# Two fixed places for keys and one for values instead of three in turn, in a cached attention step with a gated feed-forward

## The chip, the cores and the metric

The kernel runs on 1 core of one Trainium2 chip. The metric is the device time of one execution in microseconds (us). The core has a matrix engine (TensorE, PE in the profile), a vector engine (VectorE, DVE), a scalar engine (ScalarE, ACT), GpSimd (POOL), a synchronisation engine (SyncE, SP) that here only starts transfers, and 16 DMA engines that move the data. The on-chip memory has 128 partitions; a "place" below is 64 KB in each of them, 8 MB in all.

## What is computed

One decoding step: for two sequences (B = 2) with one new token each, attention over a cache of 4096 keys and values in 16 heads of 256 numbers, and beside it a feed-forward layer; a gate mixes the two.

```
q = (x @ wq).reshape(B, 1, 16, 256).transpose(0, 2, 1, 3)
scores = einsum("bhqd,bhkd->bhqk", q, k_cache) * 256 ** -0.5
p = softmax(scores);  o = einsum("bhqk,bhkd->bhqd", p, v_cache)
a = o.transpose(0, 2, 1, 3).reshape(B, 1, 4096) @ wo
h = relu(x @ w1 + b1) ** 2;  b = h @ w2 + b2
g = sigmoid((x * gate_w).sum(-1));  out = g * a + (1 - g) * b
```

All numbers are 32-bit floats. The two caches hold 134 MB each; x has 448 numbers per sequence, wq is 448 x 4096, wo is 4096 x 448, w1 is 448 x 1792 and w2 is 1792 x 448.

## The kernel before

The attention is done in 16 **rounds**. A round is a pair of heads `t` (0 to 7) of one sequence `b` (0 or 1), in the order (0,0), (0,1), (1,0) and so on. The keys of a round are 2 x 4096 rows of 256 numbers; laid over 128 partitions, 64 keys in each, they fill one place, and so do the values of the round. Each cache tensor is moved once.

**Places.** A pool `ring` with three places (L51) is handed out in turn, one place for each call of `place` (L62), whatever is to be put there: wq, the keys of round 0, wf (w1 and w2 together), the keys of round 1, and then values and keys alternately. The order of the calls thus fixes which tile follows which in a place: the values of round r come into the place of the keys of round r, and the keys of round r+2 into the place of the values of round r-1. A load into a place waits until the last reader of what stood there is done. All large loads are issued by SP, in the order of the program; a load that waits holds up those behind it. The DMA engines take the issued loads in order. ACT issues two small loads, `pack` (x, the gate's weights and b1 in 28 columns, L83) and b2 (L88), on a queue of its own.

**Start.** wq comes in two loads (L80), the keys of round 0 and of round 1 in four loads each (`cut4`, L84), wf in two (L89, L90). PE multiplies x with wq (`project_q`, L151), and `make_q(r)` (L166) spreads the q of one round over the partitions.

**A round** (loop from L278). `scores(r)` (L179): DVE multiplies the keys with q in place (L184) and sums over the 256 numbers (L185), in quarters for rounds 0 and 1, whole after that. Then SP issues the values of this round (L281), and PE makes q of the next one. `values(r - 1)` (L217) has PE multiply the weights p of the round before with its values in 64 steps; after every second round `turn` (L226) brings the result, with its normalisation, into columns `oT` that can be multiplied with wo. Then the keys of round r+2 are issued (L295), and `softmax(r)` (L187) takes the maximum, spreads it by PE, and has ACT make p. `norm` (L205) works out the normalisation after every second round. In round 0 `ffn` (L245), the feed-forward layer, follows the softmax.

**End.** wo is loaded in five pieces of 16, 8, 4, 3 and 1 blocks (`cuts`, L277) into the place of the last keys. Each block of 128 rows is multiplied with its `oT` columns. The first 28 blocks are added by `add` (L139) into the accumulator `acc`, which holds four partial sums in four groups of rows. ACT copies `acc` to `ya` (L314). The last four blocks (`LATE = 4`, L135) go by `late` (L145) straight into a second accumulator `fin`, after `ya` has been folded into it with the selection matrix `pick` (L315); `wide` (L119, L312) holds their `oT` columns spread out. ACT copies `fin` to `y4` (L318), and SP stores it (L319).

Of the kernel before, what the change touches and what calls it, by code (L numbers as in the profile page):

```python
# [19 lines left out]
def kernel(  # L20
# [24 lines left out]
    DQ = D // 4  # L45
    PLACE = KEYS * DH
    W = 17
    scale = DH ** -0.5

    const = ctx.enter_context(tc.tile_pool(name="const", bufs=1))  # L50
    ring = ctx.enter_context(tc.tile_pool(name="ring", bufs=3))  # L51
    work = ctx.enter_context(tc.tile_pool(name="work", bufs=2))
    solo = ctx.enter_context(tc.tile_pool(name="solo", bufs=1))
    ps = ctx.enter_context(tc.tile_pool(name="ps", bufs=2, space=PSUM))
# [4 lines left out]
    rounds = [(t, b) for t in range(T) for b in range(B)]  # L59
    R = len(rounds)  # L60

    def place(name):  # L62
        return ring.tile([P, PLACE], F32, name=name, tag="ring")

    def load(t, src, lo, hi):
        nc.sync.dma_start(t[:, lo:hi], src[:, lo:hi])  # L66

    def load_kv(cache, r, name, cuts=()):
        t, b = rounds[r]
        tl = place(f"{name}{r}")  # L70
        src = cache[b, 2 * t:2 * t + 2].rearrange("h (p j) d -> (h p) (j d)", j=KEYS)
        at = [0, *cuts, KEYS]
        for lo, hi in zip(at, at[1:]):
            load(tl, src, lo * DH, hi * DH)
        return tl.rearrange("p (j d) -> p j d", d=DH)

    kt, vt = {}, {}

    wqt = place("wq")
    for lo, hi in ((0, 2 * N), (2 * N, 3 * N + N // 2)):  # L80
        load(wqt, wq, lo, hi)
    pk = const.tile([P, 28], F32, name="pk")
    nc.scalar.dma_start(pk, pack)  # L83
    cut4 = (KEYS // 4, KEYS // 2, 3 * KEYS // 4)  # L84
    kt[0] = load_kv(k_cache, 0, "k", cut4)
    wft = place("wf")
    b2r = wft[0:1, PLACE - D:]
    nc.scalar.dma_start(b2r, b2)  # L88
    load(wft, wf, 0, CF * F + F // 2)  # L89
    load(wft, wf, CF * F + F // 2, CF * F + F // 2 + FC * D)  # L90
    kt[1] = load_kv(k_cache, 1, "k", cut4)

    ident = const.tile([P, P], F32, name="ident")
    make_identity(nc, ident)
# [9 lines left out]
    fin = ps1.tile([P, 512], F32, name="fin")  # L104
# [11 lines left out]
    pick = const.tile([P, W], F32, name="pick")  # L116
    nc.vector.memset(pick, 0.0)
    nc.vector.tensor_copy(pick[:, 0:W:16], m8[:, :2])
    wide = const.tile([P, 4, W], F32, name="wide")  # L119
    nc.vector.memset(wide, 0.0)  # L120

    xT = pk[:, :10].rearrange("p (c b) -> p c b", b=B)
# [12 lines left out]
    LATE = 4  # L135
    n_acc = 1 + FC + T * 4 - LATE
    added = [0]

# [6 lines left out]
    def late(lt, rhs, start=False, stop=False):  # L145
        for k in range(4):
            nc.tensor.matmul(fin[32 * k:32 * k + W, :DQ], lt, rhs[:, k * DQ:(k + 1) * DQ], start=start, stop=stop)  # L147
# [16 lines left out]
    q_sb = {}  # L164
# [11 lines left out]

    s_t = {}

    def scores(r, cuts=()):  # L179
        s_t[r] = work.tile([P, KEYS], F32, name=f"s{r}", tag="s")  # L180
        at = [0, *cuts, KEYS]
        for lo, hi in zip(at, at[1:]):
            k = kt[r][:, lo:hi, :]
            nc.vector.tensor_tensor(k, k, q_sb[r].unsqueeze(1).to_broadcast([P, hi - lo, DH]), op=ALU.mult)  # L184
            nc.vector.tensor_reduce(s_t[r][:, lo:hi], k, axis=AX.X, op=ALU.add)  # L185

    def softmax(r):  # L187
        t, b = rounds[r]
        m = work.tile([P, 1], F32, name=f"m{r}", tag="m")
        nc.vector.tensor_reduce(m, s_t[r], axis=AX.X, op=ALU.max)  # L190
        mt = ps.tile([P, 512], F32, name=f"mt{r}", tag="sm")
        nc.tensor.matmul(mt[:, :P], m.to_broadcast([P, P]), ident, start=True, stop=True)  # L192
        nb = work.tile([P, 1], F32, name=f"nb{r}", tag="nb")
        for hh in range(2):
            z = slice(64 * hh, 64 * hh + 64)
            nc.vector.tensor_reduce(nb[z], mt[z, z], axis=AX.X, op=ALU.max, negate=True)  # L196
# [41 lines left out]

    def o_block(t, k):
        hh, j = divmod(k, 2)  # L240
        return oT[t][:, j, :, hh]
# [3 lines left out]
    def ffn():  # L245
        ph = ps.tile([P, 512], F32, name="ph", tag="pq")
        for c in range(CF + 1):
            for n in range(4):
                if c < CF:
                    lt, at = xT[:, c, :], c * F + n * D  # L250
                else:
                    half, m = divmod(n, 2)
                    lt, at = xT[:, CF + half, :], CF * F + m * D
                nc.tensor.matmul(ph[32 * n:32 * n + B, :D], lt, wft[:, at:at + D], start=(c == 0), stop=(c == CF))  # L254
        w2_at = CF * F + F // 2
        h_at = w2_at + FC * D
# [12 lines left out]
        add(gP[0:1, 1, :], b2r)  # L269
        for c in range(FC):  # L270
            add(hT[:, c, :], wft[:, w2_at + c * D:w2_at + (c + 1) * D])

    project_q()
    make_q(0)
    half15 = (KEYS // 2, 3 * KEYS // 4, 7 * KEYS // 8)
    blocks = [(t, k) for t in WO_ORDER for k in range(4)]
    cuts = (0, 16, 24, 28, 31, 32)  # L277
    for r, (t, b) in enumerate(rounds):  # L278
        scores(r, cut4 if r < 2 else ())
        if r < R - 1:  # L280
            vt[r] = load_kv(v_cache, r, "v")  # L281
            make_q(r + 1)
        else:
            wot = place("wo")
            for lo, hi in zip(cuts, cuts[1:]):
                load(wot, wo, lo * D, hi * D)
        if r > 0:
            values(r - 1)
            if b == 0:
                turn(t - 1)  # L290
        if r == 0:
            softmax(r)
            ffn()
        if r + 2 < R:
            kt[r + 2] = load_kv(k_cache, r + 2, "k")  # L295
        elif r + 2 == R:
            vt[R - 1] = load_kv(v_cache, R - 1, "v", half15)
        if r > 0:
            softmax(r)
        if b == B - 1:  # L300
            norm(t)
    values(R - 1)
    turn(T - 1)
    for i, (t, k) in enumerate(blocks):
        rhs = wot[:, i * D:(i + 1) * D]
        if i < len(blocks) - LATE:
            add(o_block(t, k), rhs)
            continue
        n = i - (len(blocks) - LATE)
        if n == 0:  # L310
            for kk in range(LATE):
                nc.vector.tensor_copy(wide[:, kk, 0:W:16], o_block(t, kk))  # L312
            ya = const.tile([P, D], F32, name="ya")
            nc.scalar.activation(ya, acc[:, :D], AF.Copy)  # L314
            late(pick, ya, start=True)  # L315
        late(wide[:, n, :], rhs, stop=n == LATE - 1)
    y4 = const.tile([P, DQ], F32, name="y4")
    nc.scalar.activation(y4, fin[:, :DQ], AF.Copy)  # L318
    nc.sync.dma_start(out.rearrange("b s (k n) -> k (b s) n", k=4), y4[0:P:16, :])  # L319


# [58 lines left out]
```

## Time and profile before

| | us |
|---|---|
| median of 3 runs | 684.85 |
| fastest and slowest of the three | 683.78 and 685.77 |
| the profiled execution's own time | 685.27 |
| its span in the profile | 683.5 |
| DVE busy | 572.1 |
| PE busy | 216.6 |
| ACT busy | 33.2 |

The trace covers the span; the profiled execution's own time lies 1.8 us above it. Busy shares are averages over the span. Times in the rows of the trace are counted from the span's start. A line number is that of the code of the kernel that the row belongs to. A transfer's time to landing runs from its issue, so it holds the time in the queue as well.

### The profile page before, as it was taken

What the parts mean: (1) busy time and instruction counts of PE and PEld (TensorE: products, weight loads), DVE (VectorE), ACT (ScalarE), POOL (GpSimd) and SP (SyncE); (2) the same over time, 40 slices, a digit from 0 to 9 for tenths busy, and PEclk for the clock granted to TensorE, in tenths of its full rate; (3) what the DMA queues carried; (4) which work ended last, traced back from release to release, by engine and by line L of the source; (5) the groups of instructions that cost most, each with busy time, mean ns of one, the idle gap of its engine ahead of it and who ended that gap; (6) DMA issues with size and microseconds to landing.
All of it is one profiled execution on the core that took longest, in us unless ns stands there. A gap on an engine that the chain in (4) does not pass through costs nothing.

```text
span 683.5 us, 3411 instructions
## 1 busy us (share of the span) xinstructions
PE 216.6 (32%) x1452; PEld 62.5 (9%) x1452; DVE 572.1 (84%) x148; ACT 33.2 (5%) x107; POOL 0.7 (0%) x6
## 2 busy tenths in 40 slices
PE   2304441150515133060514215061412406050366
PEld 0001100010101001010100101010100101010012
DVE  2595895979989798989989798997979799897950
ACT  0101000010000000010000100000000100000000
POOL 0000000000000000000000000000000000000000
PEclk9756766565657556575656656575755756575579
DMA  9999999999999999999999999999999999999996
GB/s 383 420 435 423 434 433 454 445 437 426 427 403 433 433 434 430 430 431 433 433 426 434 433 433 433 437 427 418 434 414 433 395 433 434 422 430 419 419 425 278
DMA packets 7372, 289.77 MB, mean 424 GB/s; under 512 B 957, under 2 KB 1086, under 8 KB 1342
## 3 DMA queue, kind: packets, MB, share of 16 engines
q1 hardware_dynamic: 7212, 289.54, 98.9%
q8 instruction: 11, 0.18, 0.1%
q10 hardware_dynamic: 146, 0.02, 0.0%
q14 instruction: 3, 0.02, 0.0%
HBM read 289.55 MB, written 0.00 MB: 424 GB/s over the span
## 4 chain that ended last, share of the span: by engine, by line
DMA 50%; DVE 46%; PE 2%; issue 1%; ACT 0%; SPq 0%; DVEq 0%; ACTq 0%
DMA k<-in_k_cache_dram 47%; DVE s L185 23%; DVE k L184 23%; DMA wo<-in_wo_dram 3%; PE acc L142 1%; PE ph L254 1%; PE pt L263 0%; DVE m L190 0%; SPq L66 0%; PE mt L192 0%; PE fin L147 0%; ACT p L200 0%; ACT ya L314 0%; ACT wf L259 0%; DVEq L184 0%
## 5 line engine op out<-in xcount | busy, mean ns | idle before, releaser
L184 DVE TENSOR_TENSOR k<-k,q 128x16384 f32<-128x16384 f32 (+1 forms) x22 | 276.5, 12568 | 41.8 <-DMA k<-in_k_cache_dram 31.4
L185 DVE TENSOR_REDUCE s<-k 128x64 f32<-128x16384 f32 (+1 forms) x22 | 276.4, 12566 | 0.8
L223 PE MATMUL po<-v,p 128*8 128x512 f32 x1024 | 147.2, 740 | 318.8 <-DMA v<-in_v_cache_dram 318.8
L223 PEld LDWEIGHTS po<-v,p 128*8 128x8 f32 x1024 | 29.4, 104 | 433.1 <-issue 262.7
L192 PE MATMUL mt<-ident,m 128*128 128x128 f32 x32 | 12.0, 477 | 111.0 <-DVE m L190 111.0
L200 ACT ACTIVATE p<-s,nb 64x64 f32<-64x64 f32 x32 | 11.2, 350 | 368.1 <-DVE nb L196 367.7
L196 DVE TENSOR_REDUCE nb<-mt 64x1 f32<-64x64 f32 x32 | 7.1, 222 | 15.3 <-PE mt L192 14.8
L192 PEld LDWEIGHTS mt<-ident,m 128*128 128x128 f32 x32 | 7.8, 303 | 119.0 <-issue 82.7
L172 PE MATMUL pq<-qs,ident 128*64 128x256 f32 x64 | 16.0, 600 | 0.0
L228 ACT ACTIVATE o<-po 128x512 f32<-128x512 f32 x8 | 4.8, 597 | 216.4 <-PE po L223 216.4
L210 DVE RECIPROCAL rc<-sum 128x4 f32<-128x4 f32 x8 | 1.5, 183 | 11.0 <-PE sum L207 11.0
L234 PE MATMUL ot<-rl,o 128*128 128x4 f32 x64 | 8.4, 255 | 6.2 <-ACT o L228 6.2
L234 PEld LDWEIGHTS ot<-rl,o 128*128 128x128 f32 x64 | 7.7, 191 | 13.7 <-ACT o L228 13.7
L160 PE MATMUL po<-wq,pk 128*2 128x512 f32 x64 | 8.6, 683 | 1.3 <-DMA wq<-in_wq_dram 1.3
L207 PE MATMUL sum<-rsm,ones 128*128 128x4 f32 x16 | 4.5, 351 | 10.3 <-ACT p L200 10.3
L125 DVE TENSOR_TENSOR y<-pk 128x8 f32<-128x8 f32 x1 | 0.2, 168 | 9.1 <-DMA pk<-in_pack_dram 9.1
L175 ACT ACTIVATE q<-pq 128x256 f32<-128x256 f32 x16 | 6.1, 383 | 20.4 <-PE pq L172 20.2
L265 DVE TENSOR_TENSOR hb<-pt,pk 128x28 f32<-128x28 f32 x1 | 0.2, 188 | 8.1 <-PE pt L263 8.1
L142 PE MATMUL acc<-wo,oT 128*2 128x448 f32 x56 | 5.8, 538 | 1.1 <-DMA wo<-in_wo_dram 1.1
L200 ACT ACTIVATION_READ_ACCUMULATOR p<-s,nb 64x1 f32 x32 | 5.9, 184 | 0.0
L207 PEld LDWEIGHTS sum<-rsm,ones 128*128 128x128 f32 x16 | 3.8, 294 | 12.6 <-ACT p L200 12.6
L142 PE MATMUL acc<-wf,hT 128*2 128x448 f32 x28 | 4.9, 812 | 0.1
(49 smaller groups left out, 45.0 us busy)
## 6 DMA issues: line engine op xcount, KB each, us to landing
k<-in_k_cache_dram SPq DMA_DIRECT2D x8, 2048.0 KB, 35.7
wf<-in_wf_dram SPq DMA_DIRECT2D x2, 3136.0 KB, 37.8
wq<-in_wq_dram SPq DMA_DIRECT2D x1, 4096.0 KB, 12.2
v<-in_v_cache_dram SPq DMA_DIRECT2D x1, 4096.0 KB, 33.5
wo<-in_wo_dram SPq DMA_DIRECT2D x1, 3584.0 KB, 13.7
wq<-in_wq_dram SPq DMA_DIRECT2D x1, 3072.0 KB, 19.1
v<-in_v_cache_dram SPq DMA_DIRECT2D x1, 2048.0 KB
v<-in_v_cache_dram SPq DMA_DIRECT2D x2, 1024.0 KB, 40.8
```

What stands on the lines that cost most here:

```text
L142: nc.tensor.matmul(acc[32 * g:32 * g + B, :D], lt, rhs, start=n < 4, stop=n >= n_acc - 4)
L160: nc.tensor.matmul(po_bufs[a][32 * gq:32 * gq + B, :], lt, wqt[:, at:at + QB], start=(c == 0), stop=(c == CF))
L172: nc.tensor.matmul(pq[64 * hh:64 * hh + 64, :DH], ident[:, row:row + 1].to_broadcast([P, 64]), qs[:, a, hh * DH:(hh + 1) * DH], start=True ...
L184: nc.vector.tensor_tensor(k, k, q_sb[r].unsqueeze(1).to_broadcast([P, hi - lo, DH]), op=ALU.mult)
L185: nc.vector.tensor_reduce(s_t[r][:, lo:hi], k, axis=AX.X, op=ALU.add)
L192: nc.tensor.matmul(mt[:, :P], m.to_broadcast([P, P]), ident, start=True, stop=True)
L196: nc.vector.tensor_reduce(nb[z], mt[z, z], axis=AX.X, op=ALU.max, negate=True)
L200: nc.scalar.activation(p8[b][z, :, c:c + 3:2], s_t[r][z].rearrange("p (m s) -> p m s", s=2), AF.Exp, bias=nb[z], accum_out=rsm[t % 2][z, h ...
L207: nc.tensor.matmul(sm[:, :4], ones.to_broadcast([P, P]), rsm[t % 2].rearrange("p h b -> p (h b)"), start=True, stop=True)
L223: nc.tensor.matmul(po[g:g + 8, :], p8[b][:, m, :], v[:, m, :], start=(b == 0 and m < 4), stop=(b == B - 1 and m >= NM - 4))
L234: nc.tensor.matmul(ptv[:, j, :], o[:, at:at + P], rl_t[t][:, s].rearrange("p b h -> p (b h)"), start=(s == 0), stop=(s == 1))
L254: nc.tensor.matmul(ph[32 * n:32 * n + B, :D], lt, wft[:, at:at + D], start=(c == 0), stop=(c == CF))
```

## The change

- The pool `ring` with three places becomes a pool `keys` with two and a pool `vals` with one. wq, all keys and the values of the last round take turns in `keys`; wf, the values of rounds 0 to 14 and wo follow one another in the one place of `vals`. The memory taken is the same.
- The order of the issues in a round changes with it: the values of round r are issued after `values(r - 1)`, which frees their place, and then the keys of round r+2. wo is issued after `values(14)`. The load of the keys of round 1 moves behind `project_q` and `make_q(0)` in the program.
- wq comes in one load, the keys of rounds 0 and 1 in one load each, the last values in two (three quarters and one) instead of four. `pack` is loaded in two halves and b2 in four pieces.
- `scores` is split into `times_q` and `row_sums`, both over the whole tile; in round 0 `ffn` stands between them and the softmax comes after them.
- `LATE` becomes 8: 24 blocks of wo go into `acc`, eight straight into `fin`. The spread columns for all eight are made ahead of the additions. The first late block starts `fin`, and `ya` is folded in after four of them. The last copy of `fin` is made by DVE instead of ACT.

```diff
-    ring = ctx.enter_context(tc.tile_pool(name="ring", bufs=3))
+    keys = ctx.enter_context(tc.tile_pool(name="keys", bufs=2))
+    vals = ctx.enter_context(tc.tile_pool(name="vals", bufs=1))
...
-    wqt = place("wq")
-    for lo, hi in ((0, 2 * N), (2 * N, 3 * N + N // 2)):
-        load(wqt, wq, lo, hi)
+    wqt = place(keys, "wq")
+    load(wqt, wq, 0, 3 * N + N // 2)
     pk = const.tile([P, 28], F32, name="pk")
-    nc.scalar.dma_start(pk, pack)
-    cut4 = (KEYS // 4, KEYS // 2, 3 * KEYS // 4)
-    kt[0] = load_kv(k_cache, 0, "k", cut4)
-    wft = place("wf")
+    for z in (slice(0, 14), slice(14, 28)):
+        nc.scalar.dma_start(pk[:, z], pack[:, z])
+    kt[0] = load_kv(k_cache, 0, keys, "k")
+    wft = place(vals, "wf")
     b2r = wft[0:1, PLACE - D:]
-    nc.scalar.dma_start(b2r, b2)
+    for k in range(4):
+        nc.scalar.dma_start(b2r[:, k * DQ:(k + 1) * DQ], b2[:, k * DQ:(k + 1) * DQ])
     load(wft, wf, 0, CF * F + F // 2)
     load(wft, wf, CF * F + F // 2, CF * F + F // 2 + FC * D)
-    kt[1] = load_kv(k_cache, 1, "k", cut4)
...
-    def scores(r, cuts=()):
+    def times_q(r):
+        nc.vector.tensor_tensor(kt[r], kt[r], q_sb[r].unsqueeze(1).to_broadcast([P, KEYS, DH]), op=ALU.mult)
+
+    def row_sums(r):
         s_t[r] = work.tile([P, KEYS], F32, name=f"s{r}", tag="s")
...
+        nc.vector.tensor_reduce(s_t[r], kt[r], axis=AX.X, op=ALU.add)
...
     project_q()
     make_q(0)
-    half15 = (KEYS // 2, 3 * KEYS // 4, 7 * KEYS // 8)
+    kt[1] = load_kv(k_cache, 1, keys, "k")
...
     for r, (t, b) in enumerate(rounds):
-        scores(r, cut4 if r < 2 else ())
+        times_q(r)
         if r < R - 1:
-            vt[r] = load_kv(v_cache, r, "v")
             make_q(r + 1)
-        else:
-            wot = place("wo")
-            for lo, hi in zip(cuts, cuts[1:]):
-                load(wot, wo, lo * D, hi * D)
+        if r == 0:
+            ffn()
+        row_sums(r)
         if r > 0:
             values(r - 1)
             if b == 0:
                 turn(t - 1)
-        if r == 0:
-            softmax(r)
-            ffn()
+        if r < R - 1:
+            vt[r] = load_kv(v_cache, r, vals, "v")
+        else:
+            wot = place(vals, "wo")
+            for lo, hi in zip(cuts, cuts[1:]):
+                load(wot, wo, lo * D, hi * D)
         if r + 2 < R:
-            kt[r + 2] = load_kv(k_cache, r + 2, "k")
+            kt[r + 2] = load_kv(k_cache, r + 2, keys, "k")
         elif r + 2 == R:
-            vt[R - 1] = load_kv(v_cache, R - 1, "v", half15)
-        if r > 0:
-            softmax(r)
+            vt[R - 1] = load_kv(v_cache, R - 1, keys, "v", (3 * KEYS // 4,))
+        softmax(r)
...
+    early = len(blocks) - LATE
+    for n, (t, k) in enumerate(blocks[early:]):
+        nc.vector.tensor_copy(wide[:, n, 0:W:16], o_block(t, k))
     for i, (t, k) in enumerate(blocks):
...
         if n == 0:
-            for kk in range(LATE):
-                nc.vector.tensor_copy(wide[:, kk, 0:W:16], o_block(t, kk))
             ya = const.tile([P, D], F32, name="ya")
             nc.scalar.activation(ya, acc[:, :D], AF.Copy)
-            late(pick, ya, start=True)
-        late(wide[:, n, :], rhs, stop=n == LATE - 1)
+        if n == LATE // 2:
+            late(pick, ya)
+        late(wide[:, n, :], rhs, start=n == 0, stop=n == LATE - 1)
     y4 = const.tile([P, DQ], F32, name="y4")
-    nc.scalar.activation(y4, fin[:, :DQ], AF.Copy)
+    nc.vector.tensor_copy(y4, fin[:, :DQ])
```

More of the change, by code (lines that the diff above doesn't have):

```diff
@@ L60, with place, load_kv @@
     R = len(rounds)
-    def place(name):
-        return ring.tile([P, PLACE], F32, name=name, tag="ring")
+    def place(pool, name):
+        return pool.tile([P, PLACE], F32, name=name, tag="place")
     def load(t, src, lo, hi):
         nc.sync.dma_start(t[:, lo:hi], src[:, lo:hi])
-    def load_kv(cache, r, name, cuts=()):
+    def load_kv(cache, r, pool, name, cuts=()):
         t, b = rounds[r]
-        tl = place(f"{name}{r}")
+        tl = place(pool, f"{name}{r}")
         src = cache[b, 2 * t:2 * t + 2].rearrange("h (p j) d -> (h p) (j d)", j=KEYS)
@@ L118 @@
     nc.vector.tensor_copy(pick[:, 0:W:16], m8[:, :2])
-    wide = const.tile([P, 4, W], F32, name="wide")
+    LATE = 8
+    wide = const.tile([P, LATE, W], F32, name="wide")
     nc.vector.memset(wide, 0.0)
@@ L133 @@
     nc.vector.tensor_scalar(gP[:, 1, :], gP[:, 0, :], -1.0, 1.0, op0=ALU.mult, op1=ALU.add)
-    LATE = 4
     n_acc = 1 + FC + T * 4 - LATE
@@ L177 @@
     s_t = {}
-    def scores(r, cuts=()):
+    def times_q(r):
+        nc.vector.tensor_tensor(kt[r], kt[r], q_sb[r].unsqueeze(1).to_broadcast([P, KEYS, DH]), op=ALU.mult)
+    def row_sums(r):
         s_t[r] = work.tile([P, KEYS], F32, name=f"s{r}", tag="s")
[L181 to L185, printed above, removed]
+        nc.vector.tensor_reduce(s_t[r], kt[r], axis=AX.X, op=ALU.add)
     def softmax(r):
@@ L303 @@
     turn(T - 1)
+    early = len(blocks) - LATE
+    for n, (t, k) in enumerate(blocks[early:]):
+        nc.vector.tensor_copy(wide[:, n, 0:W:16], o_block(t, k))
     for i, (t, k) in enumerate(blocks):
         rhs = wot[:, i * D:(i + 1) * D]
-        if i < len(blocks) - LATE:
+        if i < early:
             add(o_block(t, k), rhs)
             continue
-        n = i - (len(blocks) - LATE)
+        n = i - early
         if n == 0:
-            for kk in range(LATE):
-                nc.vector.tensor_copy(wide[:, kk, 0:W:16], o_block(t, kk))
             ya = const.tile([P, D], F32, name="ya")
             nc.scalar.activation(ya, acc[:, :D], AF.Copy)
-            late(pick, ya, start=True)
-        late(wide[:, n, :], rhs, stop=n == LATE - 1)
+        if n == LATE // 2:
+            late(pick, ya)
+        late(wide[:, n, :], rhs, start=n == 0, stop=n == LATE - 1)
     y4 = const.tile([P, DQ], F32, name="y4")
-    nc.scalar.activation(y4, fin[:, :DQ], AF.Copy)
+    nc.vector.tensor_copy(y4, fin[:, :DQ])
     nc.sync.dma_start(out.rearrange("b s (k n) -> k (b s) n", k=4), y4[0:P:16, :])
```

## The prediction

> **What bounds the kernel now.** The page comes first, for the busy shares, the DMA queue and the summary of the chain.
>
> ```profile
> span 683.5 us, 3411 instructions
> DMA  9999999999999999999999999999999999999996
> GB/s 383 420 435 423 434 433 454 445 437 426 427 403 433 433 434 430 430 431 433 433 426 434 433 433 433 437 427 418 434 414 433 395 433 434 422 430 419 419 425 278
> q1 hardware_dynamic: 7212, 289.54, 98.9%
> DMA 50%; DVE 46%; PE 2%; issue 1%; ACT 0%; SPq 0%; DVEq 0%; ACTq 0%
> ```
>
> SP's queue is busy for 98.9% of the span, and the 289.54 MB are the caches and weights, each once. So the transfers are the bound, although the chain gives DVE 46%: DVE stands there because its last read of a place starts the next load. What can be won is the difference between a full stream and this one. For the full stream I take the timeline of PE, where the multiplication with values starts when they land, and the windows.
>
> ```profile
> 95.15 8.80 PE L223 MATMUL po<-v,p 128*8 128x512 f32 x64 [18.60 <-DMA v<-in_v_cache_dram]
> 133.88 9.91 PE L223 MATMUL po<-v,p 128*8 128x512 f32 x64 [24.44 <-DMA v<-in_v_cache_dram]
> 95.15:133.88 38.73, 10.40 (x72) 2.54 (x73) 31.51 (x12) 1.26 (x5) 0.00 (x0) 0.63 1.00 434
> 133.88:172.50 38.62, 12.79 (x78) 3.63 (x78) 35.05 (x6) 2.03 (x7) 0.00 (x0) 0.59 1.01 435
> ```
>
> Two places, keys 2 and values 1, land between 95.15 and 133.88: 19.365 us for one place at 434 GB/s. That is my price of an 8192 KB transfer. The chain of waits gives the landing of keys 2, keys 14 and the 28th block of wo, as start plus duration.
>
> ```profile
> 76.06 38.41 DMA k<-in_k_cache_dram
> 540.91 43.21 DMA k<-in_k_cache_dram
> 658.24 19.36 DMA wo<-in_wo_dram
> ```
>
> Keys 2 land at 114.48 (start and duration are rounded), keys 14 at 584.12. Between them 24 places are moved in 469.64 us; at 19.365 they need 464.76, so 4.9 us are lost. From 584.12 to 677.60 four places and 28 of the 32 blocks of wo (6272 KB, 14.83 us) need 92.29 us and take 93.48: 1.2 lost. Together **6.1 us**. Where they go is seen in the issues of SP (timeline) and in windows of 7.26 us after them, the time of three 64 KB rows on one DMA engine.
>
> ```profile
> 106.23 0.33 SPq L66 DMA_DIRECT2D v<-in_v_cache_dram  x1
> 149.11 0.33 SPq L66 DMA_DIRECT2D v<-in_v_cache_dram  x1
> 618.75 3.13 SPq L66 DMA_DIRECT2D v<-in_v_cache_dram  x5
> 106.23:113.49 7.26, 1.59 (x8) 0.79 (x8) 1.24 (x7) 1.26 (x5) 0.00 (x0) 0.69 1.00 433
> 187.79:195.05 7.26, 2.40 (x8) 1.30 (x8) 4.09 (x8) 1.26 (x5) 0.00 (x0) 0.50 0.90 361
> 265.83:273.09 7.26, 2.41 (x8) 1.30 (x8) 4.15 (x8) 1.26 (x5) 0.00 (x0) 0.50 0.92 389
> 304.69:311.95 7.26, 1.82 (x6) 0.80 (x6) 3.39 (x4) 1.26 (x5) 0.00 (x0) 0.50 1.01 433
> 618.75:626.01 7.26, 0.77 (x2) 0.50 (x2) 3.80 (x4) 0.87 (x4) 0.00 (x0) 0.50 1.00 380
> ```
>
> At 106.23 the transfer under way still had 8.3 us to go (keys 2 land at 114.48), and the window holds 433 GB/s. From 149.11 on, the last reader of a place ends only some 4 us before the stream runs out: values 1 land at 133.88, so keys 3 land at 153.2, 4.1 us after the issue. In the windows after such issues the rate is 361, 389, 433 and 380. My reading is that the 16 DMA engines do not end together; the quick ones are through before the new load reaches them, and begin it cold. Thirteen issues (149.11 to 618.75) have this short lead; 6.1 us over them is 0.47 us each.
>
> **The change part by part.**
>
> *Places.* The same bytes move in the same order: keys r+1, values r, keys r+2. What changes is when a load may start. Values r now wait for PE to finish with values r-1, keys r+2 for DVE to finish with keys r. Values r-1 land, PE needs 8.8 to 9.9 us (rows above), and beside it keys r+1 are moving for 19.4 us; so values r are issued 9.5 to 10.6 us before the stream would run out. DVE ends a round about 34.5 us after its keys land (17.2 us for each pass, rows below); keys r+2 are wanted 58.1 us (three places) after that: 23 us of lead.
>
> ```profile
> L184 DVE TENSOR_TENSOR k<-k,q 128x16384 f32<-128x16384 f32 x14 | 241.2, 17225 | 31.1 <-DMA k<-in_k_cache_dram 20.7 <-issue 10.4
> L185 DVE TENSOR_REDUCE s<-k 128x64 f32<-128x16384 f32 x14 | 241.1, 17220 | 0.5
> ```
>
> Both leads are longer than the 8.3 us that cost nothing. SP waits in the order values r, keys r+2, and behind each wait stand only loads wanted later. I take back 5.1 of the 6.1 us: I keep 1 us as loss not tied to the issues, a choice between the ends 0 and 6.1. **-5.1**.
>
> [...]
>
> *Start.* wq is whole when its second half was, and DVE starts later. The rows:
>
> ```profile
> 25.27 4.43 DVE L184 TENSOR_TENSOR k<-k,q 128x4096 f32<-128x4096 f32 x1 [10.70 <-DMA k<-in_k_cache_dram]
> wq<-in_wq_dram SPq DMA_DIRECT2D x1, 3072.0 KB, 19.1
> pk<-in_pack_dram ACTq DMA_DIRECT2D x1, 14.0 KB, 12.4
> L160 PE MATMUL po<-wq,pk 128*2 128x512 f32 x64 | 8.6, 683 | 1.3 <-DMA wq<-in_wq_dram 1.3
> PE 216.6 (32%) x1452; PEld 62.5 (9%) x1452; DVE 572.1 (84%) x148; ACT 33.2 (5%) x107; POOL 0.7 (0%) x6
> DVE nb L196 <- PE mt L192: 14.8, 16, 1.0
> DVE rc L210 <- PE sum L207: 11.0, 8, 1.4
> 24.00:76.00 52.00, 15.38 (x102) 6.18 (x103) 41.43 (x17) 5.63 (x12) 0.00 (x0) 0.61 1.01 431
> ```
>
> wq lands at about 20.3 (its second load is issued about 1.2), `project_q` runs about 21 to 30 instead of starting on half of wq, and the first DVE multiplication moves from 25.3 to the landing of keys 0 at about 39.7. What hides those 14 us: all of DVE's work with its waits for PE is 572.1 + 14.8 + 11.0 = 598 us, so from 39.7 it could be done at 638, while the values of the last round, by the sum above, come at about 656. If that cover were gone, each us of late start would count in full. Keys 1 wait for `project_q` at about 31; wf holds the queue until about 54.5. `ffn` on DVE and PE falls into the wait between the two DVE passes of round 0, and frees the place of values 0 at about 63, with keys 1 moving until about 74: 11 us of lead. Fewer, longer rows in place of quarters: the stretch 24:76 ran at 431 against 434, which is 0.36 us; I take **-0.35** (ends 0 and 0.36).
>
> The small loads on ACT's queue: `pack` took 12.4 us to land, about as long as the first half of wq beside it, so it was served row by row in turn with that. Whole rows of wq will let its first half land with wq, at about 20, and the second half, which only the feed-forward bias needs, at about 40; b2 follows by about 47. Nobody waits: the bias is wanted after the first DVE pass, at about 57. If a later large load has to wait for one of these small ones, keys 1 would be issued at up to 47 instead of 31, still 7.5 us ahead of the end of wf. **0**, with 0.5 (one short lead) as the upper end and 0 as the lower. [...]
>
> *End.* The rows of the timeline and the issue table:
>
> ```profile
> 657.38 2.23 SPq L66 DMA_DIRECT2D wo<-in_wo_dram  x5
> wo<-in_wo_dram SPq DMA_DIRECT2D x1, 224.0 KB, 20.6
> 677.64 0.93 PE L142 MATMUL acc<-wo,oT 128*2 128x448 f32 x8 [0.41 <-DMA wo<-in_wo_dram]
> 679.44 0.95 PE L147 MATMUL fin<-wo,wide 128*17 128x112 f32 x32
> 680.45 0.26 ACT L318 ACTIVATE y<-fin 128x112 f32<-128x112 f32 x1 [1.27 <-PE fin L147]
> L147 PE MATMUL fin<-wo,wide 128*17 128x112 f32 x32 | 1.0, 259 | 0.0
> L312 DVE COPY wide<-oT 128x2 f32<-128x2 f32 x4 | 0.4, 164 | 0.0
> 2.05 0.48 DVE L103 MEMSET acc<- 128x512 f32 x1
> 679.23 0.39 PE L147 MATMUL fin<-ya,pick 128*17 128x112 f32 x8 [0.66 <-ACT ya L314]
> ```
>
> Now the 28th block (677.6) starts a chain of additions, `ya`, `pick` and the four late blocks to 680.45, while the last block lands at about 659.2 + 20.6 = 679.8. After the change `ya` needs only 24 blocks and is folded in while the last pieces land; behind the last landing stand four products of `fin` (eight matmuls in the trace, two for each): 0.42 us (0.26 for the last, seven starts ahead of it at 0.022, as 32 take 0.95). That is 680.2, so **-0.25**. The copy by DVE instead of ACT: no row has it. DVE's smallest copy takes 0.16 us, its clear of a wider tile of the same memory 0.48; I take the 0.26 that ACT needed, between them: 0, ends -0.1 and +0.2. Eight spread copies instead of four lie beside the loading of wo. wo is issued after `values(14)`, again about 10 us ahead.
>
> Sum: 685.27 - 5.1 - 0.35 - 0.25 = 679.6 for an execution like the profiled one. That one is 0.42 above the median of the three, so the median is forecast at **679.1**.
>
> **The rivals.**
>
> *A. The dips belong to the round's end itself, not to the lead* (the softmax between two DVE passes, the pair of issues). Then they stay, and only 0.6 us are won: 684.3. For it: the dips stand where DVE turns from one round to the next. Against it: 106.23 is such a place too, and its window holds 433.
>
> *B. Every issue costs, whatever the lead,* because setting up 128 rows slows the rows under way. Place: each issue that falls into a full stream. The pair is now issued together; the change pulls it apart into two moments per round, so the 0.47 us come twice as often: +6.1, less 0.6, is 690.4 in the median. It decides as soon as a lone issue costs as much as a pair. Against it: the windows 95.15:133.88 and 133.88:172.50, which hold the issues from 106.23 to 149.11, run at 434 and 435.
>
> *C. PE frees the place of the values too late.* It decides when PE ends with values r-1 more than 19.4 us after they land; it takes 9.9. Each us beyond that costs 14 us in 14 rounds, so 2 us late would give 707. In the rows PE waits for the values, never they for PE, and nothing stands ahead in its order but the next q.
>
> **How the numbers follow.** Forecast, gain of 4 to 7 us: 0.62. The same way but smaller, 2 to 4 us: 0.14. A: 0.14. B: 0.07. C: 0.03. A measurement of this kernel tells 0.3%, 2.05 us, from no change. Faster 0.76, same 0.14, slower 0.10. The lower end: all 6.1, 0.36, 0.35 and a run 1 us below its median (the three lie from 1.1 below to 0.9 above) give 677.0. The upper end takes in A: 684.4. B and C stay out. The forecast's own range is 677.0 to 681.
>
> **What would show it.** Right: values and keys issued at separate times, values r about 10 us before keys r+1 land; windows of 7.26 us after the issues at 430 or more; values landing every 38.7 to 38.8 us; DVE idle before L184 grown, since it waits for keys each round; first DVE pass at about 40; keys 14 landing near 579; the store about 0.42 us plus a copy after the last landing. Wrong: the rate still dips in each round although the lead is 10 us (A), dips after both issues (B), or PE's multiplication with values starting well after their landing (C).

## The result and the profile after

The change makes the kernel 0.7% faster: median 680.25 us (680.04 to 680.45 in six runs) against 684.64 (683.78 to 685.77, six runs). The ratio is 0.9934, with a 95% interval of 0.9921 to 0.9947. The profiled execution took 680.04 us, its span is 678.3.

From the page of the kernel after, the span, the rate of the transfers in 40 slices, and the shares of the chain that ended last:

```profile
span 678.3 us, 3450 instructions
GB/s 379 445 420 436 433 433 434 433 433 433 434 433 433 437 433 434 433 434 433 433 437 438 433 433 433 434 433 433 434 441 433 433 433 430 433 433 433 420 420 260
q1 hardware_dynamic: 5916, 289.54, 98.9%
DMA 76%; PE 23%; issue 0%; SPq 0%; ACT 0%; DVE 0%
DMA v<-in_v_cache_dram 65%; PE po L222 20%; DMA wf<-in_wf_dram 4%; DMA wo<-in_wo_dram 4%; DMA pk<-in_pack_dram 3%; PE acc L142 1%; PE ph L253 1%; PE pt L262 1%; SPq L67 0%; PE fin L147 0%; ACT wf L258 0%; DVE y L319 0%
```

The bytes and the busy share of the queue are those of before. What is new is the evenness: before, the slices went down to 395 and 403 GB/s; now nearly all of the middle ones read 433 or 434. A busy share of 98.9% in both kernels does not show the difference, because a row that takes longer, up to 4.2 us instead of 2.42 in the kernel before, counts as busy for longer (rows are followed one by one below). DVE has all but left the chain: the loads now follow PE, which frees the place of the values.

The issues of SP in the kernel after, and the windows of 7.26 us behind them (columns: stretch, its length, busy time of PE, its weight loads, DVE, ACT and POOL, granted clock, DMA share, GB/s):

```profile
219.94 0.33 SPq L67 DMA_DIRECT2D v<-in_v_cache_dram  x1
225.91 0.33 SPq L67 DMA_DIRECT2D k<-in_k_cache_dram  x1
...
608.86 6.59 SPq L67 DMA_DIRECT2D v<-in_v_cache_dram  x3
```

```profile
187.18:194.44 7.26, 2.41 (x8) 1.30 (x8) 4.28 (x8) 1.26 (x5) 0.00 (x0) 0.50 1.00 433
219.94:227.20 7.26, 1.98 (x12) 1.70 (x14) 6.27 (x3) 0.78 (x2) 0.00 (x0) 0.86 1.00 433
614.65:621.91 7.26, 0.77 (x2) 0.50 (x2) 3.72 (x4) 0.87 (x4) 0.00 (x0) 0.50 1.00 433
```

Values and keys are issued apart, and all three windows hold 433, among them those at 187.18 and 614.65, where DVE turns from one round to the next. In the DVE timeline of the kernel after, keys land 10.2 us after the issue at 219.94:

```profile
39.78 17.23 DVE L180 TENSOR_TENSOR k<-k,q 128x16384 f32<-128x16384 f32 x1 [17.90 <-DMA k<-in_k_cache_dram]
230.11 17.22 DVE L180 TENSOR_TENSOR k<-k,q 128x16384 f32<-128x16384 f32 x1 [2.55 <-DMA k<-in_k_cache_dram]
580.13 17.23 DVE L180 TENSOR_TENSOR k<-k,q 128x16384 f32<-128x16384 f32 x1 [1.67 <-DMA k<-in_k_cache_dram]
```

Where the time came from is read at three marks: the start of PE on values 0, on values 14, and the last copy of `fin`. First PE and DVE after, then the one row of before that the prediction did not show:

```profile
94.64 9.16 PE L222 MATMUL po<-v,p 128*8 128x512 f32 x64 [16.71 <-DMA v<-in_v_cache_dram]
638.26 8.72 PE L222 MATMUL po<-v,p 128*8 128x512 f32 x64 [22.48 <-DMA v<-in_v_cache_dram]
674.36 0.96 PE L147 MATMUL fin<-wo,wide 128*17 128x112 f32 x32 [0.49 <-DMA wo<-in_wo_dram]
675.38 0.28 DVE L319 COPY y<-fin 128x112 f32<-128x112 f32 x1 [17.74 <-PE fin L147]
```

```profile
643.11 9.59 PE L223 MATMUL po<-v,p 128*8 128x512 f32 x64 [23.23 <-DMA v<-in_v_cache_dram]
```

| stretch | before | after | won |
|---|---|---|---|
| start, to values 0 | 95.15 | 94.64 | 0.51 |
| values 0 to values 14, 28 places | 547.96 | 543.62 | 4.34 |
| values 14 to the last copy | 37.34 | 37.12 | 0.22 |
| sum, to the last copy | 680.45 | 675.38 | 5.07 |

The medians differ by 4.4 us, less than these 5.1, because the profiled execution of before (685.27) lies 0.63 us above its median and that of after (680.04) 0.21 us below its own.

### The profile page after: what moved, and what is told of

It reads as the page before. It is cut to its first block, busy times and chain, and to the rows that moved or that the text cites. A ratio compares the mean times of both kernels' runs of the same rounds, so it can differ in the third digit from the quotient of the medians.

```text
span 678.3 us, 3450 instructions
## 1 busy us (share of the span) xinstructions
PE 222.3 (33%) x1476; PEld 65.5 (10%) x1476; DVE 571.3 (84%) x141; ACT 32.9 (5%) x106; POOL 0.7 (0%) x6
## 3 DMA queue, kind: packets, MB, share of 16 engines
q1 hardware_dynamic: 5916, 289.54, 98.9%
## 4 chain that ended last, share of the span: by engine, by line
DMA 76%; PE 23%; issue 0%; SPq 0%; ACT 0%; DVE 0%
DMA v<-in_v_cache_dram 65%; PE po L222 20%; DMA wf<-in_wf_dram 4%; DMA wo<-in_wo_dram 4%; DMA pk<-in_pack_dram 3%; PE acc L142 1%; PE ph L253 1%; PE pt L262 1%; SPq L67 0%; PE fin L147 0%; ACT wf L258 0%; DVE y L319 0%
## 5 line engine op out<-in xcount | busy, mean ns | idle before, releaser
L180 DVE TENSOR_TENSOR k<-k,q 128x16384 f32<-128x16384 f32 x16 | 275.6, 17225 | 38.5 <-DMA k<-in_k_cache_dram 38.5
L184 DVE TENSOR_REDUCE s<-k 128x64 f32<-128x16384 f32 x16 | 275.5, 17219 | 0.5
L253 PE MATMUL ph<-wf,pk 128*2 128x448 f32 x32 | 5.1, 804 | 14.9 <-DMA wf<-in_wf_dram 14.9
```

Of the source, the lines that this page charges most:

```text
L180: nc.vector.tensor_tensor(kt[r], kt[r], q_sb[r].unsqueeze(1).to_broadcast([P, KEYS, DH]), op=ALU.mult)
L184: nc.vector.tensor_reduce(s_t[r], kt[r], axis=AX.X, op=ALU.add)
```

## The experiments

The theory, called the lead theory here: what counts is the **lead**, that is how long before the stream of transfers runs out the next load is issued. The theory says that with about 4 us some of the 16 DMA engines have already run dry, and that with more they have not. The rivals: the dips belong to the round's end (A); every issue costs (B); the loss comes when two loads are issued as a pair; or start and end of the kernel carry the gain. The runs of one group share the runs of the kernel before, whose median was 686.01, 685.92 and 685.90 us in the three groups. The stretch from values 0 to values 14 in the trace is given beside the time, since it holds what the lead can change.

**Places alone.** The kernel before with the two pools and the new order of issues; start in quarters and end as before.

```diff
-    ring = ctx.enter_context(tc.tile_pool(name="ring", bufs=3))
+    keys = ctx.enter_context(tc.tile_pool(name="keys", bufs=2))
+    vals = ctx.enter_context(tc.tile_pool(name="vals", bufs=1))
...
-        if r == 0:
-            softmax(r)
-            ffn()
+        if r < R - 1:
+            vt[r] = load_kv(v_cache, r, vals, "v")
```

> The kernel before with the two pools and the new order of issues alone; start in quarters and the end as before (the feed-forward stands behind the score passes of round 0 so that its place is free in time). Lead theory (a load that is issued only about 4 us before the stream runs out loses 0.3 us): values land every 38.7 us and the time is 680.9, 3.7 us under the kernel before. Rival, that the start and the end carry the gain: within 1 us of the kernel before, 684.

Measured: 681.17 us, ratio 0.9933 (0.9914 to 0.9952). PE starts on values 0 and 14:

```profile
95.21 10.00 PE L223 MATMUL po<-v,p 128*8 128x512 f32 x64 [26.79 <-DMA v<-in_v_cache_dram]
638.84 9.55 PE L223 MATMUL po<-v,p 128*8 128x512 f32 x64 [22.48 <-DMA v<-in_v_cache_dram]
```

543.63 us, the stretch of the changed kernel to a hundredth. The places alone give what the whole change gives, within the intervals. Start and end show only beside other runs with long leads: the medians of those below that have the new start and end and their loads in the same pieces lie at 680.15 to 680.57 us, against 681.17 here, and the 0.73 us that the traces above give to start and end agree with that.

**All the rest alone.** The ring of three with the new start and end.

```diff
-    for lo, hi in ((0, 2 * N), (2 * N, 3 * N + N // 2)):
-        load(wqt, wq, lo, hi)
+    load(wqt, wq, 0, 3 * N + N // 2)
...
-        scores(r, cut4 if r < 2 else ())
+        scores(r)
...
+    LATE = 8
```

> The kernel before with all of the change but the places: whole loads at the start, pack and b2 in pieces, last values in two, eight late blocks, last copy by DVE. Lead theory: the three places still issue with 4 us of lead, so only start and end are won, 0.5 and 0.2 us: 683.9. Rival, that start and end carry the gain: 680.5.

Measured: 695.18 us, ratio 1.0132 (1.0111 to 1.0153): 9 us *slower*, which neither theory had expected. The timeline from the end of round 0 shows why:

```profile
74.22 0.33 SPq L66 DMA_DIRECT2D v<-in_v_cache_dram  x1
...
85.81 0.19 DVE L265 TENSOR_TENSOR hb<-pt,pk 128x28 f32<-128x28 f32 x1 [10.00 <-PE pt L263]
...
92.12 0.33 SPq L66 DMA_DIRECT2D k<-in_k_cache_dram  x1
97.28 8.74 PE L223 MATMUL po<-v,p 128*8 128x512 f32 x64 [4.67 <-DMA v<-in_v_cache_dram]
...
121.08 0.33 SPq L66 DMA_DIRECT2D v<-in_v_cache_dram  x1
...
143.04 7.17 PE L223 MATMUL po<-v,p 128*8 128x512 f32 x40 [17.95 <-DMA v<-in_v_cache_dram]
```

Keys 0 come whole at 39.7, so DVE is 14 us late; then it waits 10 us for the feed-forward layer, which here, as in the kernel before, stands behind the softmax (8.1 us there). In the ring, values 1 go into the place of keys 1 and wait for DVE, until 121.08. Values 0 had landed at 97.28 and keys 2, the only load queued behind them, are moved by about 116.7 (19.4 us): the stream stood empty. From values 0 to values 1 it takes 45.8 us instead of 38.7, 7 of the 9 us. The other 2 were lost ahead of it: values 0, issued at 74.22 instead of 60.54, land at 97.28 instead of 95.15. The late start of DVE, which costs nothing with the new places, has no cover in the old ones.

**The end alone.** To part start from end, the kernel before with the new end only.

```diff
-            vt[R - 1] = load_kv(v_cache, R - 1, "v", half15)
+            vt[R - 1] = load_kv(v_cache, R - 1, "v", (3 * KEYS // 4,))
...
-    LATE = 4
+    LATE = 8
```

> The kernel before with the changed end alone (last values in two loads, eight late blocks, last copy by DVE), start in quarters. 0.2 to 0.5 us under the kernel before, not to be told from it by its time; so what made start and end together slower in the ring of three, 9 us, is the start. If the end were to blame: 9 us over it.

Measured: 686.07 us, ratio 0.9994 (0.9978 to 1.0010). No difference that can be told, so the 9 us belong to the start. The 0.2 us that the end may win are below what these runs resolve.

**A short lead in the new places.** DVE clears one number of the place of values 1 to 14 after the sums of the round; the load behind it has to wait for that.

```diff
         tl = place(pool, f"{name}{r}")
+        if held:
+            nc.vector.memset(tl[0:1, 0:1], 0.0)
...
-            vt[r] = load_kv(v_cache, r, vals, "v")
+            vt[r] = load_kv(v_cache, r, vals, "v", held=r > 0)
```

> The changed kernel, but DVE clears one number of the place of the values after the sums of round r, so that values 1 to 14 are issued about 4 us before the stream runs out, as in the kernel before; places and all else as changed. Lead theory: the loss comes back, 14 times 0.3 us: 684.5. Rival A, the loss belongs to the round's end or to the ring of three: as the changed kernel, 680.3. Rival of the pair (the loss comes when two loads are issued together): 684.5 too, as keys follow at once.

Measured: 686.55 us, ratio 0.9999 (0.9982 to 1.0017): the whole gain is gone. An issue and the landing of the keys after it, 4.2 us later:

```profile
227.75 0.33 SPq L67 DMA_DIRECT2D v<-in_v_cache_dram  x1
```

```profile
231.94 17.23 DVE L182 TENSOR_TENSOR k<-k,q 128x16384 f32<-128x16384 f32 x1 [2.57 <-DMA k<-in_k_cache_dram]
```

```profile
94.71 9.08 PE L224 MATMUL po<-v,p 128*8 128x512 f32 x64 [16.83 <-DMA v<-in_v_cache_dram]
644.39 9.01 PE L224 MATMUL po<-v,p 128*8 128x512 f32 x64 [22.90 <-DMA v<-in_v_cache_dram]
```

Values 0 to 14 take 549.68 us, 6.06 more than in the changed kernel, 0.43 for each of the 14 issues. In the kernel before it was 4.34 over 13 short leads, 0.33 each.

**A shorter one.** The same, with the load behind the softmax in the program.

```diff
-        if r < R - 1:
-            vt[r] = load_kv(v_cache, r, vals, "v", held=r > 0)
...
         softmax(r)
+        if r < R - 1:
+            vt[r] = load_kv(v_cache, r, vals, "v", held=r > 0)
```

> As the run with 4 us of lead, but values r are issued after the softmax of round r, about 2 us before the stream runs out. Lead theory: the loss grows, to about 1 us each or 14 us: 694 (688 to 705). Rival A: 680.3. Rival of the pair: 684.5, no more than with 4 us.

Measured: 698.12 us, ratio 1.0176 (1.0152 to 1.0200). The issue, the landing of the keys (3.1 us later, not 2, since the transfers are late themselves), and PE on values 0 and 14:

```profile
231.67 0.33 SPq L67 DMA_DIRECT2D v<-in_v_cache_dram  x1
```

```profile
234.80 17.23 DVE L182 TENSOR_TENSOR k<-k,q 128x16384 f32<-128x16384 f32 x1 [3.19 <-DMA k<-in_k_cache_dram]
```

```profile
94.50 9.50 PE L224 MATMUL po<-v,p 128*8 128x512 f32 x64 [16.41 <-DMA v<-in_v_cache_dram]
656.36 8.47 PE L224 MATMUL po<-v,p 128*8 128x512 f32 x64 [25.86 <-DMA v<-in_v_cache_dram]
```

That is 561.86 us, 18.24 more than in the changed kernel: 1.3 for each issue. Keys follow at once in both runs, so the pair is the same and the loss is three times as large. Rival A expected no loss in either, and falls with them; the rival of the pair falls with the second.

**Longer leads.** The sums are split, and the number is cleared between the parts: behind 56 of the 64 columns, then behind 48.

```diff
+        row_sums(r, 0, KEYS - 8)
...
+            vt[r] = load_kv(v_cache, r, vals, "v", held=r > 0)
...
+        row_sums(r, KEYS - 8, KEYS)
```

> As the run with 4 us of lead, but the number is cleared after 56 of the 64 columns of the sums, the other 8 being summed behind it: values are issued about 6 us before the stream runs out, and apart from the keys, which follow some 2 us later. Lead theory: between the kernels, 681 to 683, as most of the 16 engines still have work. Rival of the pair: 680.3, as no two loads are issued together.

> The same, cleared after 48 of the 64 columns: about 8 us of lead. Lead theory: 680.3, as the changed kernel, since the issue with 8 us of lead in the kernel before cost nothing. If a waiting DVE cost something by itself: 682 or more.

Measured: 680.57 us, ratio 0.9921 (0.9899 to 0.9943), and 680.47, ratio 0.9922 (0.9902 to 0.9942). In the first the issue comes 6.3 us ahead, and the window behind it is full:

```profile
224.42 0.33 SPq L67 DMA_DIRECT2D v<-in_v_cache_dram  x1
```

```profile
230.74 17.23 DVE L182 TENSOR_TENSOR k<-k,q 128x16384 f32<-128x16384 f32 x1 [2.49 <-DMA k<-in_k_cache_dram]
```

```profile
224.42:231.68 7.26, 1.81 (x6) 0.79 (x6) 3.75 (x5) 1.26 (x5) 0.00 (x0) 0.54 1.00 433
```

The issue and the landing of the keys in the second, 8.4 us apart, and PE on values 0 and 14 in the first and in the second:

```profile
221.91 0.33 SPq L67 DMA_DIRECT2D v<-in_v_cache_dram  x1
```

```profile
230.36 17.23 DVE L182 TENSOR_TENSOR k<-k,q 128x16384 f32<-128x16384 f32 x1 [2.48 <-DMA k<-in_k_cache_dram]
```

```profile
94.90 8.92 PE L225 MATMUL po<-v,p 128*8 128x512 f32 x64 [17.55 <-DMA v<-in_v_cache_dram]
638.51 8.48 PE L225 MATMUL po<-v,p 128*8 128x512 f32 x64 [22.41 <-DMA v<-in_v_cache_dram]
```

```profile
94.47 8.45 PE L225 MATMUL po<-v,p 128*8 128x512 f32 x64 [16.26 <-DMA v<-in_v_cache_dram]
638.11 9.69 PE L225 MATMUL po<-v,p 128*8 128x512 f32 x64 [22.42 <-DMA v<-in_v_cache_dram]
```

The stretches are 543.61 and 543.64 us. I had expected a part of the loss at 6 us; there is none.

| lead of the issue shown | values 0 to 14 | loss for each issue |
|---|---|---|
| 3.1 us | 561.86 | 1.30 |
| 4.2 us | 549.68 | 0.43 |
| 6.3 us | 543.61 | 0 |
| 8.4 us | 543.64 | 0 |
| 10.2 us (changed kernel) | 543.62 | - |

In each run the lead varies from issue to issue, since keys that are late themselves lengthen it: from values 2 on it is 2.4 to 5.8 us, 3.2 to 5.7, 5.9 to 7.2, 6.4 to 9.3 and 9.3 to 11.7. In the run with the shortest, leads of 2.4 to 2.7 us alternate from values 7 on with leads of 5.0 to 5.8, and the steps from one tile of values to the next, 41.1 to 41.5 us and 38.9 to 39.7, alternate with them. The execution traced at 4.2 us was 1.4 us above the median of its runs; by the medians of this run and of that with 6.3 us, 5.98 us apart, the loss is 0.43 for each issue again.

In both short runs the keys follow the values at once. The kernel before has one such pair with a long lead, with the issue at 106.23 (lead 8.3 us) and keys behind it:

```profile
106.66 0.38 SPq L66 DMA_DIRECT2D k<-in_k_cache_dram  x1
```

It loses nothing: values 1 land 38.73 us after values 0. A single load with a short lead was not tried.

What is lost behind a short lead can be read in the traces row by row. The trace keeps the time of nearly every row of 64 KB that a DMA engine moves; in the full stream it is 2.42 us. A window gives the mean: its bytes over 65,536 are its rows, and its DMA share times 16 engines times its length is their time. So the window at 187.79 of the kernel before (0.90 and 361 GB/s) holds 40 rows of 2.61 us, and this one, of the run with 3.1 us of lead, 35 rows of 2.8 us:

```profile
270.83:278.09 7.26, 1.64 (x6) 0.80 (x6) 3.73 (x5) 1.23 (x5) 0.00 (x0) 0.50 0.85 317
```

Between values 0 and 14 the changed kernel has 10 rows of more than 2.5 us, the kernel before 165, the runs with 4.2 and 3.1 us of lead 185 and 246, most of them less than 5 us after an issue. Shared out among 16 engines, the time by which rows were longer than in the changed kernel is 3.9 of the 4.3 us lost in the kernel before, 4.7 of 6.1 with 4.2 us of lead and 7.1 of 18.2 with 3.1; the rest is time in which engines stood idle. So at 4 us only a small part of the loss is engines that have run dry, as the theory had it; for the most part the rows behind a late issue take longer, up to 4.2 us in the kernel before. Idle engines are the larger part only at 3 us. Why such a row takes longer is not shown.

**The old ring with a long lead.** The kernel before without the multiplication by q, so that DVE is early.

```diff
-            nc.vector.tensor_tensor(k, k, q_sb[r].unsqueeze(1).to_broadcast([P, hi - lo, DH]), op=ALU.mult)
```

> The kernel before without the multiplication of keys with q (left out: the scores are sums of the keys alone), so that DVE ends a round some 17 us earlier; ring of three, pairs of issues and places as before. Lead theory: leads of about 20 us, values land every 38.7 us, about 5 us under the kernel before. Rival A, the round's end, the pair and the ring of three: as the kernel before.

Measured: 681.40 us, ratio 0.9934 (0.9914 to 0.9953). Values are issued at 170.91, some 21 us before the stream would run out, and PE starts on values 0 and 14 at

```profile
95.53 9.87 PE L222 MATMUL po<-v,p 128*8 128x512 f32 x64 [30.10 <-DMA v<-in_v_cache_dram]
639.24 9.38 PE L222 MATMUL po<-v,p 128*8 128x512 f32 x64 [26.64 <-DMA v<-in_v_cache_dram]
```

543.71 us in the three places of before. So it is not where a tile lies, nor how many places there are, but when the load is issued. Of the pair this run says nothing, although it was expected to keep it: with DVE early, the keys are issued 10.9 us behind the values.

```profile
170.91 0.33 SPq L66 DMA_DIRECT2D v<-in_v_cache_dram  x1
181.78 0.33 SPq L66 DMA_DIRECT2D k<-in_k_cache_dram  x1
```

**DVE as a load on the memory.** The changed kernel without the same multiplication.

```diff
-        nc.vector.tensor_tensor(kt[r], kt[r], q_sb[r].unsqueeze(1).to_broadcast([P, KEYS, DH]), op=ALU.mult)
+        pass
```

> The changed kernel without the multiplication of keys with q (left out: the scores are sums of the keys alone), so DVE has half its work and no writes into the places of the keys. If the stream of loads alone is the bound now and DVE takes nothing from it: as the changed kernel, within 0.5 us of 680.3. Rival, that DVE's reads and writes of the same memory slow the stream: 2 us or more faster.

Measured: 680.15 us, ratio 0.9907 (0.9888 to 0.9927). With half of DVE's work gone nothing is won: the stretch is 543.62 us again. The stream is the bound, and DVE takes nothing from it.

**Twice the issues.** Keys and values in two halves of each row.

```diff
-            vt[r] = load_kv(v_cache, r, vals, "v")
+            vt[r] = load_kv(v_cache, r, vals, "v", (KEYS // 2,))
```

> The changed kernel with keys 2 to 15 and values 0 to 14 loaded in two halves each: twice the issues, leads as long as before. Lead theory: as the changed kernel, 680.3. Rival B, each issue costs: 29 more issues at 0.3 us and more, 689.

Measured: 683.01 us, ratio 0.9955 (0.9939 to 0.9971), 2.4 us over the median of the run with 6 us of lead beside it. PE begins on the second halves of values 0 and 14:

```profile
94.57 5.32 PE L222 MATMUL po<-v,p 128*8 128x512 f32 x32 [4.31 <-DMA v<-in_v_cache_dram]
...
640.55 5.32 PE L222 MATMUL po<-v,p 128*8 128x512 f32 x32 [4.24 <-DMA v<-in_v_cache_dram]
```

545.98 us, 2.36 more than in the changed kernel for 28 more loads: 0.084 each. So a load, or its shorter rows, has a small price although the lead is long; rival B has at most a grain of truth, at a fifth of the price it needed.

**Load or row?** The same number of loads, but halves by partitions, with rows of 64 KB.

```diff
-            load(tl, src, lo * DH, hi * DH)
+            for z in range(rows):
+                at_p = slice(z * P // rows, (z + 1) * P // rows)
+                nc.sync.dma_start(tl[at_p, lo * DH:hi * DH], src[at_p, lo * DH:hi * DH])
```

> As the run with halves, 28 or 29 more loads, but each half takes 64 of the 128 partitions, so that the rows stay 64 KB long. If each load costs about 0.09 us in a full stream: again 2.5 us over the changed kernel, 683. If it was the shorter rows of 32 KB: 680.3.

Measured: 1291.75 us, ratio 1.8815 (1.8776 to 1.8855). The question is not answered, because something else took over. A window in the middle:

```profile
200.00:300.00 100.00, 21.53 (x146) 5.69 (x138) 36.13 (x11) 3.29 (x12) 0.00 (x0) 0.60 0.99 205
```

The DMA engines are busy for 0.99 of the time and move 205 GB/s, less than half. That run leaves the question open whether the 0.084 us belong to the load or to the row; the traces speak for the row. In the run with halves the median row of 32 KB takes 1.216 us, and half of the median row of 64 KB in the changed kernel is 1.2105. The 0.0055 us between them, times the 448 half rows of one engine, are 2.5 us, about all of the 2.36.

**Fewer loads at the end.** The changed kernel with the last values in one load and wo in four pieces.

```diff
-    cuts = (0, 16, 24, 28, 31, 32)
+    cuts = (0, 16, 24, 31, 32)
```

> The changed kernel with two loads fewer at the end: last values in one, wo in four pieces (blocks 24 to 30 together). By 0.09 us for a load 680.1, not to be told from the changed kernel by its time; if PE now waits at the end, up to 1 us slower.

Measured: 682.17 us, ratio 0.9937 (0.9918 to 0.9955); 2.0 over the median of the run without the multiplication beside it. PE begins on the last values and on `fin` later than in the changed kernel (656.32 and 674.36 there):

```profile
658.18 9.48 PE L222 MATMUL po<-v,p 128*8 128x512 f32 x64 [1.14 <-DMA v<-in_v_cache_dram]
...
669.43 4.69 PE L142 MATMUL acc<-wo,oT 128*2 128x448 f32 x48
...
675.84 0.96 PE L147 MATMUL fin<-wo,wide 128*17 128x112 f32 x32
676.86 0.27 DVE L319 COPY y<-fin 128x112 f32<-128x112 f32 x1 [18.56 <-PE fin L147]
```

PE has to wait 1.14 us for the last values, and everything behind it is late; from values 14 (638.91) to the copy it takes 37.95 us instead of 37.12. That is 0.83 of the 2.0 us. PE was 0.66 us late at values 0 already (95.30), ahead of anything that was changed, and the profiled execution lies 3.1 us above its span (682.99 and 679.9) where that of the changed kernel lies 1.7 above; why is not known. Together two loads fewer are no gain. No version that I tried and that does the whole computation beats the changed kernel.

## Why the prediction was right

*Places, -5.1.* Right in mechanism, a little too large: 4.34 us were won between values 0 and values 14. The lead of values r was forecast at 9.5 to 10.6 us; it is 10.2. Where the forecast put the point was from 106.23 in the kernel before, a lead of 8.3 us; the runs put it between 4.2 and 6.3. What was mis-sized is the loss "not tied to the issues". I kept 1 us of 6.1. By my own price of a full transfer, 28 places need 542.2 us, and the kernel after takes 543.62, so 1.4 remain in this stretch alone. 1.0 of them is one step: from values 12 to values 13 it takes 39.80 us instead of 38.6 to 39.0 as elsewhere, and the runs with long leads have the step at the same place. So keys 14 land at 580.13 and not near 579. The trace shows what stands there. The DMA engines also carry the program's instructions, which are a queue of the page:

```profile
q8 instruction: 11, 0.18, 0.1%
```

One of these packets, of 16 KB, takes an engine 1.07 us at 563.5, and the row behind it takes 2.91 us. The trace keeps 16 landings for each large load; from keys 14 on the last of them comes 1.2 us later behind the others than before. The other long-lead runs have such a packet between 563.4 and 564.5 us too. Packets at 298.4 and 426.8 fall into steps 0.2 us longer than the turn of 38.63 and 38.81 us that the others keep; the rest delay engines that are not the last. That fits the 1.4 us, but no run was made to test it.

One sign failed: DVE was to wait longer for its keys.

```profile
L180 DVE TENSOR_TENSOR k<-k,q 128x16384 f32<-128x16384 f32 x16 | 275.6, 17225 | 38.5 <-DMA k<-in_k_cache_dram 38.5
```

Less the 17.90 of round 0, it waits 20.6 us instead of 31.1. It had waited in every round before; now it comes too late to wait in round 2 (5.2 us before), and the rounds became shorter (4.9 us from round 2 to 15).

*Behind a late issue.* Behind the issue at 121.08 of the run with the rest alone, into an empty stream, the 16 engines begin their first rows 0.9 to 1.7 us later; behind the first issue of the changed kernel, at 0.74, it is 1.0 to 1.8 us. That time is no measure of the lead that the stream needs here: at 4.2 us each issue loses 0.43 us, at 6.3 us none. Two more things are in the traces. The first rows behind the issue at 121.08 take 2.7 to 3.6 us instead of 2.42, so the prediction's words that the engines begin a late load cold fit. And the engines do not end together: the first of the 16 landings of a load comes 1.8 to 2.2 us ahead of the last in the changed kernel, from keys 1 to values 12. The runs show how the loss grows as the lead shrinks; how the two things make it up is argued.

*Start, -0.35.* Measured 0.51. Single executions differ by nearly as much: PE starts on values 0 at 94.5 to 95.3 us in those traced above with whole loads at the start and the new places, at 95.0 to 95.5 in those with quarters. The rows above show the first DVE pass at 39.78 (forecast 39.7), and it cost nothing. The whole loads were priced as a small gain in both rivals and forecast; the run with the rest alone shows what the cover was worth that the prediction named: without the new places the same start costs 9 us. The run with halves gives an estimate of what fewer rows are worth: 896 fewer up to values 0, 56 for each engine, at 0.0055 us are 0.3 us, of the size that was forecast. The small loads did hold up a large one, as allowed for: keys 1 were issued at 39.96, with the second half of `pack`, and not at 31; wf was still moving, with its last landing in the trace at 55.8, so nothing was lost.

*End, -0.25.* Measured 0.22, though the picture was wrong in part. I had eight matmuls behind the last landing and 0.42 us; the row at 674.36 shows 32 of them, four blocks, starting together after a landing, and 1.0 us to the copy. PE does not wait a second time there, so by then, or while those matmuls ran, the last block had landed too. DVE's copy took 0.28 us where ACT's took 0.26.

*Sum.* 5.7 forecast, 5.07 in the traces, 5.23 between the two profiled executions. The median came out at 680.25 against 679.1. Of these 1.1 us, 0.5 are the sum, in which the places were 0.8 too large and start, end and what lies outside the stretches 0.3 too small. The other 0.6 come from the last step: I took 0.42 us off for an execution above its median, and the profiled execution of the kernel after lies 0.21 below its own.

*The rivals.* A fell with the windows at 187.18 and 614.65 of the kernel after, and with the runs of leads. B keeps 0.084 us for a load instead of 0.47, and by the row times even that is the price of its shorter rows. C did not come: PE was done 10.2 us ahead.

## What to carry to other kernels

In a kernel bound by its loads, do not look at the busy share of the queue but at the rate behind each issue: a full share over the span (98.9% in both kernels) can hide a stream that is 10% slow or more for some microseconds (361 to 389 GB/s instead of 433 in three of the four windows behind short leads). Tie each place to the engine that frees it early, so that the next load is issued well before the one under way ends (here 6 us were enough and 4 were not), and test the lead by holding a load back. A change at the start that is free under one order of places can cost 9 us under another, so cost each part against the order that it will run in.

## What the runs showed of the hardware

- Loads into 64 of the 128 partitions, one half after the other, ran at 205 GB/s with a DMA share of 0.99, against 433 for loads into all 128, and the median row takes 5.13 us instead of 2.42. Why is not shown.
- A row of 64 KB took one DMA engine 2.42 us in the full stream, and up to 4.2 us behind a late issue in the kernel before. The 16 KB packet of instructions at 563.5 in the changed kernel took one engine 1.07 us.
- A short lead also makes the time uncertain: the kernel before ran from 683.67 to 688.32 in one group and the run with 4 us of lead from 683.01 to 687.92, while the runs with 6 and 8 us stayed within 1 us.
- The stretch of 28 places took 543.6 to 543.7 us in all seven runs with long leads and whole loads, with one longer step, between values 12 and 13, of 39.5 to 40.2 us. A packet of instructions stands there in the traces; that it is the cause was not tried.
